# Normalizations and weight parts on GpSimd, all loads in one queue, and a new order at the beginning of a banded attention with a gated feed-forward layer

## The chip, the cores and the metric

The kernel runs on one core of one Trainium2 chip. The metric is the device time of one execution in microseconds: 874.63 us before, the median of three runs (872.39 to 875.89).

## The reference

Attention over 8 batches, 8 heads, 576 positions and 64 dimensions, with a causal window of 64 keys, then a feed-forward layer over the 4608 tokens of 512 channels with 2048 inner ones:

```python
scores = scale * np.matmul(q, k.transpose(0, 1, 3, 2))
mask = (rel >= 0) & (rel < window)            # window = 64
scores = np.where(mask, scores, -1000000000.0)
attn = np.exp(scores - np.max(scores, axis=-1, keepdims=True))
attn = attn / (np.sum(attn, axis=-1, keepdims=True) + 1e-09)
x = np.matmul(attn, v)                        # -> 4608 x 512
h = x @ w_in                                  # 512 x 2048
g = np.where(h >= 1, h, np.where(h <= -1, 0.0, (h + 1) ** 2 / 4))
out = (g @ w_out).astype(np.float32)          # 2048 x 512
```

The weights arrive as float64, q, k and v as float32.

## The kernel before

**Tiles.** The tokens are nine tiles of 512. Each tile is four attention steps of 128 tokens (two query blocks of 64), and then 16 groups f of 128 inner channels: `ffn_in` (L909) multiplies the tile with w_in, a gate follows, `ffn_out` (L960) multiplies with w_out into four PSUM banks `acc`. Every operand of the two products is split into a high part in fp32r and a low part, the remainder; three matmuls (high x high, high x low, low x high) stand for one. Tiles 3 to 8 go in pairs, with seven products where eight would be needed (L840); that part is not touched by more than its numbers.

**Weights.** A group has two units, 0 for w_in and 1 for w_out. A unit of 128 x 512 float64 numbers is 0.5 MB (`raw`). It becomes fp32 by a chain: `w_rest` and `w_sign` on ScalarE (L329, L306), two limits, a shift and a join on VectorE (L310, L322, L333), the high part on ScalarE (`w_high`, L277), the low part on VectorE (`w_low`, L345). The first four groups are loaded in single units, the later twelve in pairs. Each weight is converted once, during tile 0.

**Attention steps.** Step s loads q, k and two v blocks. Steps 0 to 3 add the mask in PSUM by a matmul with the identity (L415), then scores (L421), maximum (L442), exponentials with sums (L449, 16 on ScalarE for the two halves h), inverse (L456, L457), normalization (`att_normalize`, L461, on VectorE for steps 0 to 7), transposes on TensorE (L485, steps 0 to 6) and copies to `ptd` (L277 or L279), then the values (L499), and a high and a low part, `xh` and `xl` (L512). Steps 7 and later transpose on VectorE. L277 and L279 are the copies of the helper `copy` on ScalarE and on VectorE.

**What sets the order.** A planner (class `Plan`) holds every piece of work with a key, a cost in ns for each engine that may do it, what it depends on, and which buffers it takes and gives back. It walks through time on its own costs: of the work that could start on an engine within `PATIENCE`, the smallest key goes first. The order in which it emits is the program order of each engine, and stays that; an engine waits for whatever stands next in its order. A piece marked `shared` does not begin while GpSimd is busy by the plan, nor the other way round. Keys come from tables of numbers: `A_FIRST` for steps 0 to 3, `W_FIRST`, `W_STEP` and `W_LATE` for the weight chain, `W0_KEY` and `W0_STEP` for the weight loads, `L_LEAD` and `V_LATE` for q, k and v.

**Buffers and queues.** q and k have two buffers each, v has four, PSUM has two banks each for `ps_a` and `ps_h`, and four for `acc`. SP issues nearly all transfers, in its program order: a load that waits for a buffer holds up every load behind it. The first k and the first weight unit are issued by ScalarE (the call of `load_k` and `w_load` before `plan.run`).

**Filling.** Eight matmuls on zeros stand at the start (`warm`, L267), and 8 and 4 ahead of the two transposes of step 0 (`FILL`, L483).

## Time and profile before

| | |
|---|---|
| median of three runs | 874.63 us |
| profiled execution | 875.65 us, span 873.8 us |
| mean granted TensorE clock | 0.996 |
| busy: TensorE / VectorE / ScalarE / GpSimd | 861.2 / 648.4 / 501.1 / 179.0 us |
| first 45 us: DMA | 191 to 424 GB/s in pieces of 5 us |
| first L909 | at 24.02 us |
| first GpSimd arithmetic after the masks | at 115.80 us |

The span runs from the first to the last instruction. TensorE's busy time counts matmuls with ends that are modelled, so a stretch of full TensorE has to be compared with the number of matmuls in it. A row of the timeline gives start and length in us, the engine, the line, the operation and the tiles; a "x16" is 16 instructions in a row, and the bracket is the idle time ahead of it and what ended it.

### The profile page before, as it was taken

The page shows a single profiled execution, that of the slowest core. Times are in us where ns is not written, and L with a number is a line of the kernel's source. Part 1 is how long each engine was busy: PE and PEld are TensorE (multiplying, and loading weights), DVE is VectorE, ACT ScalarE, POOL GpSimd, SP SyncE. Part 2 cuts the span into 40 slices and gives each one's busy share as a digit, 9 for nine tenths or more (in the row PEclk, how much of TensorE's full clock was granted, in tenths as well). Part 3 has the DMA queues.
Part 4 walks back from the last instruction along what each step waited for, and adds up shares of the span by engine and source line. Part 5 has one row for each costly group of instructions (what it writes and reads, how often), then busy time and mean ns, then how long its engine had stood idle before and what let it go on. Part 6 is the DMA issues. An engine that isn't in the chain of part 4 may idle for free.

```text
span 873.8 us, 17796 instructions
## 1 busy us (share of the span) xinstructions
PE 861.2 (99%) x6708; PEld 701.4 (80%) x6708; DVE 648.4 (74%) x1282; ACT 501.1 (57%) x1250; POOL 179.0 (20%) x194
## 2 busy tenths in 40 slices
PE   8899999999999999999999999999999999999998
PEld 6788888878787888878877888787888888888886
DVE  6899999987787776797888947888799733333453
ACT  6899976546454556545336845553548733333564
POOL 1000046656332452111111001211121011111000
PEclk9899999999999999999999999999999999999999
DMA  9992126767533314657665407677545045554321
GB/s 318 420 357 93 55 79 223 234 198 234 169 128 128 110 55 140 235 192 229 194 200 190 145 13 239 202 222 216 165 129 180 25 153 166 162 155 146 102 105 48
DMA packets 88116, 147.57 MB, mean 169 GB/s; under 512 B 7392, under 2 KB 36448, under 8 KB 88032
## 3 DMA queue, kind: packets, MB, share of 16 engines
q1 hardware_dynamic: 87600, 145.40, 50.8%
q8 instruction: 53, 0.87, 0.4%
q10 hardware_dynamic: 432, 1.05, 0.3%
q14 instruction: 31, 0.25, 0.1%
HBM read 112.86 MB, written 33.55 MB: 168 GB/s over the span
## 4 chain that ended last, share of the span: by engine, by line
PE 89%; DVE 3%; DMA 3%; ACT 2%; POOL 1%; issue 1%; SPq 0%; ACTq 0%; POOLq 0%; DVEq 0%
PE acc L960 43%; PE ps_h L840 26%; PE ps_h L909 13%; PE ps_a L499 4%; PE ps_a L421 3%; DMA kept<-u 1%; DMA vt<-in_v 1%; ACT sm L449 1%; DMA raw<-in_w 1%; DVE sm L461 1%; DVE ptd L467 0%; DVE a L934 0%; ACT u L329 0%; PE ps_a L485 0%; POOL u L778 0%
## 5 line engine op out<-in xcount | busy, mean ns | idle before, releaser
L960 PE MATMUL acc<-wts,gh 128*128 128x512 f32 x1152 | 360.0, 394 | 0.0
L960 PEld LDWEIGHTS acc<-wts,gh 128*128 128x128 f32 x1152 | 212.8, 188 | 46.8 <-issue 0.3
L960 PE MATMUL acc<-wts,gl 128*128 128x512 f32 x576 | 224.8, 390 | 0.6 <-POOL gl L944 0.6
L944 POOL TENSOR_TENSOR gl<-a,gh 128x512 fp32r<-128x512 f32 (+1 forms) x80 | 103.3, 1292 | 474.4 <-ACT gh L939 399.4
L840 PE MATMUL ps_h<-wts 128*128 128x512 f32 x720 | 180.3, 391 | 0.0
L840 PEld LDWEIGHTS ps_h<-wts 128*128 128x128 f32 x720 | 134.3, 188 | 29.1 <-DVE h L855 0.6
L467 DVE STREAM_TRANSPOSE ptd<-sm 32x256 f32<-32x256 f32 x336 | 146.5, 436 | 5.9
L939 ACT CAST gh<-a 128x512 fp32r<-128x512 f32 (+1 forms) x149 | 89.5, 601 | 89.7 <-DVE a L934 82.2
L855 DVE TENSOR_TENSOR h<-h,ps_h 128x512 f32<-128x512 f32 x120 | 82.0, 684 | 75.2 <-PE ps_h L840 73.8
L909 PE MATMUL ps_h<-xh,wts 128*128 128x512 f32 (+1 forms) x424 | 131.1, 376 | 2.7 <-DVE xh L279 1.7
L960 PEld LDWEIGHTS acc<-wts,gl 128*128 128x128 f32 x576 | 108.1, 188 | 24.3 <-POOL gl L944 1.1
L934 DVE SCALAR_TENSOR_TENSOR a<-a,h 128x512 f32<-128x512 f32 x96 | 66.7, 696 | 63.1 <-ACT a L927 61.7
L922 ACT ACTIVATE a<-h 128x512 f32<-128x512 f32 x96 | 60.3, 631 | 90.9 <-DVE h L855 61.8
L449 ACT ACTIVATE sm<-sm,nm 128x96 f32<-128x96 f32 (+1 forms) x256 | 93.1, 366 | 20.4 <-DVE nm L442 20.4
L909 PEld LDWEIGHTS ps_h<-xh,wts 128*128 128x128 f32 x424 | 78.3, 191 | 17.9 <-DVE xh L279 1.8
L927 ACT ACTIVATE a<-a 128x512 f32<-128x512 f32 (+1 forms) x139 | 85.5, 617 | 4.3
L909 PE MATMUL ps_h<-xl,wts 128*128 128x512 f32 (+1 forms) x212 | 79.1, 373 | 0.4 <-DVE xl L512 0.4
L840 PE MATMUL ps_h<-xs,wts 128*128 128x512 f32 x288 | 73.8, 392 | 0.0
L277 ACT COPY h<-ps_h 128x512 f32<-128x512 f32 x47 | 27.6, 587 | 75.0 <-PE ps_h L840 74.7
L840 PEld LDWEIGHTS ps_h<-xs,wts 128*128 128x128 f32 x288 | 53.7, 188 | 11.5
L922 ACT ACTIVATE a<-ps_h 128x512 f32<-128x512 f32 (+1 forms) x53 | 29.4, 554 | 48.9 <-PE ps_h L909 42.3
L944 DVE TENSOR_TENSOR gl<-a,gh 128x512 fp32r<-128x512 f32 (+1 forms) x69 | 45.6, 662 | 7.8 <-ACT gh L939 7.6
(109 smaller groups left out, 834.4 us busy)
## 6 DMA issues: line engine op xcount, KB each, us to landing
wts<-kept SPq DMA_DIRECT2D x168, 256.0 KB, 3.0
vt<-in_v SPq DMA_DIRECT2D x72, 256.0 KB, 3.4
kt<-in_k SPq DMA_DIRECT2D x35, 384.0 KB, 4.2
raw<-in_w SPq DMA_DIRECT2D x12, 1023.8 KB, 10.0
qt<-in_q SPq DMA_DIRECT2D x36, 256.0 KB, 3.3
spill<-h SPq DMA_DIRECT2D x18, 512.0 KB, 2.9
h<-spill SPq DMA_DIRECT2D x18, 512.0 KB, 3.5
out<-o SPq DMA_DIRECT2D x27, 256.0 KB, 2.3
```

The costliest lines, as they stand in the source:

```text
L449: nc.scalar.activation(sm[:, p, :], (ps if masked else sm)[:, p, :], AF.Exp, bias=nm[:, p:p + 1], scale=scale if masked else 1.0, accum_ou ...
L467: nc.vector.transpose(dst[:, :, r], src[:, :, c * SQ:(c + 1) * SQ])
L499: nc.tensor.matmul(ps[half[h], p, n], lhsT=vt[i][:, c:c + D], rhs=pt[h][:, p, n], start=True, stop=True)
L840: nc.tensor.matmul(ps, lhsT=r[:, part, cp], rhs=x_op(k, xp)[:, cp], start=j in (0, 1, 3, 4) and i == 0 and cp == 0, stop=j in (1, 2, 5, 6) ...
L855: nc.vector.tensor_tensor(out=h[:, to], in0=h[:, of], in1=prods[u, n, b], op=ALU.add)
L909: nc.tensor.matmul(ps, lhsT=wts[f, 0][:, part, c * P:(c + 1) * P], rhs=x[:, c, r], start=(c == 0 and j == 0), stop=(c == NP - 1 and j == 2),)
L922: nc.scalar.activation(gs[t, f, r.start][0], phs[t, f, r.start], AF.Relu, bias=0.5, scale=0.5)
L927: nc.scalar.activation(a, a, AF.Square)
L934: nc.vector.scalar_tensor_tensor(out=a, in0=a, scalar=1.0, in1=ps, op0=ALU.min, op1=ALU.max)
L939: nc.scalar.copy(g[1], g[0])
L944: engine[eng].tensor_tensor(out=g[2], in0=g[0], in1=g[1].bitcast(F32), op=ALU.subtract)
L960: nc.tensor.matmul(acc[t, i], lhsT=g[:, sub], rhs=wts[f, 1][:, part], start=(q == 0 and j == 0), stop=(q == NF - 1 and j == 2),)
```

## The change

The changed program differs in these ways. Line numbers move by 22 to 30: L909 becomes L939, L960 becomes L990, L485 becomes L509, L499 becomes L523, L421 becomes L447, L415 becomes L437, L461 becomes L487, L345 becomes L367.

- 13 normalizations of steps 0 to 6 (all but one) are given to GpSimd, and the low parts of ten weight groups: six single units and four pairs.
- The first k and the first weight unit go through SP with all the others, in a new order.
- The mask products of steps 0 to 3 are a piece of work of their own, which can stand ahead of the arrival of q and k.
- Zeroing of the identity, the masks and `ptd` moves to VectorE and ahead.
- Filling is left to the planner: six matmuls at the start, and as many as fit where it sees TensorE idle before the transposes of steps 0 and 1 and before the first products of tile 0.
- The last tile's last 128 tokens are taken from PSUM whole by ScalarE, not in two halves by VectorE and ScalarE.
- Nearly all numbers of the tables are other ones, those of the later tiles too.

```diff
-W_FIRST = (20.54, -1.96, 1.46, 0.57, -0.16)
-W_STEP = 4 / 3
-L_LEAD = 2
+W_FIRST = (-23.48, 35.42, 28.14, 28.55, 19.15)
+W_STEP = 1.78
+L_LEAD = 16.26
...
-FIRST_LOAD = 0, (0,)
+NORM_POOL = ((0, 0), (0, 1), (1, 0), (1, 1), (2, 0), (2, 1), (3, 0), (3, 1), (4, 0), (4, 1), (5, 1), (6, 0), (6, 1))
+LOW_POOL = ((0, (0,)), (0, (1,)), (1, (0,)), (2, (0,)), (3, (0,)), (3, (1,)), (6, (0, 1)), (7, (0, 1)), (9, (0, 1)), (10, (0, 1)))
...
-NWARM = 8
-FILL = 8, 4
-A_FIRST = (-102.6, -95.58, -95.43, -95)
+NWARM = 6
+FILLED = 3
+FILL_NS = 260
+FILL_SLACK = 500
+A_FIRST = (-144.83, -88.9, -110.73, -84.04)
...
+            if i in self.filled and at < FILL_UNTIL:
+                since = max([idle[e]] + [self.pools[n][turn[n]] for n in takes])
+                self.fills = n = max(0, int((at - since - FILL_SLACK) / FILL_NS))
...
-    def w_low(g):
+    def w_low(g, eng):
         t = ws[g]
-        nc.vector.tensor_tensor(out=t[:, :, 1], in0=us[g], in1=t[:, :, 0].bitcast(F32), op=ALU.subtract)
+        engine[eng].tensor_tensor(out=t[:, :, 1], in0=us[g], in1=t[:, :, 0].bitcast(F32), op=ALU.subtract)
...
-        x = add(key - W_LATE[4], dict(DVE=join), lambda e: w_join(g), [x])
+        x = add(key - W_LATE[4], dict(DVE=join), lambda e: w_join(g), [x], shared=bool(NORM_POOL + LOW_POOL))
...
+            xm = add(key, dict(PE=M_PE), lambda e: att_mask_banks(s, ps), [last["r"]], takes=[ps, ps])
+            needs.append(xm)
...
-                x = add(due + D_LATE[4], NORM[1], lambda e, h=h: att_normalize(s, h, e), [x], shared=True)
+                x = add(due + D_LATE[4], dict(Pool=830) if (s, h) in NORM_POOL else NORM[1], lambda e, h=h: att_normalize(s, h, e), [x], shared=True)
...
-        load_k(0, nc.scalar)
-        w_load(FIRST_LOAD, nc.scalar)
         plan.run()
```

TensorE around the first products of tile 0, before (idt,sm are transposes, ptd,vt values of an attention step, xh,wts the first products):

```order
L909 MATMUL ps_h<-xh,wts 128x256
L485 MATMUL ps_a<-idt,sm 128x128 x12
L499 MATMUL ps_a<-ptd,vt 64x64 x16
L485 MATMUL ps_a<-idt,sm 128x128 x4
L499 MATMUL ps_a<-ptd,vt 64x64 x16
L909 MATMUL ps_h<-xh,wts 128x256
```

The first row is the last matmul of the first block of 12; the transposes and the values of steps 2 and 3 follow, then the second block. The same place now:

```order
L523 MATMUL acc<-ptd,vt 64x64 x16
L509 MATMUL ps_a<-idt,sm 128x128 x4
L523 MATMUL ps_a<-ptd,vt 64x64 x16
L939 MATMUL ps_h<-xh,wts 128x256
...
L939 MATMUL ps_h<-xh,wts 128x256
L509 MATMUL ps_a<-idt,sm 128x128 x8
L939 MATMUL ps_h<-xh,wts 128x256
...
L939 MATMUL ps_h<-xh,wts 128x256
L523 MATMUL ps_a<-ptd,vt 64x64 x16
L990 MATMUL acc<-wts,gh 128x512 x2
```

The values of step 2 now stand ahead of the first block of 12, the second block stands ahead of the values of step 3, and L990 comes right behind these.

GpSimd's first arithmetic was the sums of weights for the later tiles:

```order
L256 MEMSET msk 64x64 x2
L761 TENSOR_TENSOR u<-wts 128x256 x2
L770 TENSOR_TENSOR u<-u 128x128 x3
L761 TENSOR_TENSOR u<-wts 128x256
L778 TENSOR_TENSOR u<-u,o 128x512
```

Now low parts (wts) and normalizations (sm) stand ahead of them:

```order
L278 MEMSET msk 64x64 x2
L367 TENSOR_TENSOR wts<-u,wts 128x512
L487 TENSOR_TENSOR sm<-sm,den 128x512 x2
L367 TENSOR_TENSOR wts<-u,wts 128x512
L487 TENSOR_TENSOR sm<-sm,den 128x512 x4
L367 TENSOR_TENSOR wts<-u,wts 128x512
L487 TENSOR_TENSOR sm<-sm,den 128x512 x2
L367 TENSOR_TENSOR wts<-u,wts 128x512 x3
L487 TENSOR_TENSOR sm<-sm,den 128x512 x2
```

The normalizations of steps 0 to 3 are the eight in the rows of two, four and two.

SP's first transfers, before (ScalarE issues the first k and the first weight unit at the same time; 128x2047 is a weight unit):

```order
L391 DMA qt_146<-in_q 128x512
L400 DMA vt_171<-in_v 128x512
L391 DMA qt_173<-in_q 128x512
L395 DMA kt_177<-in_k 128x768
L400 DMA vt_180<-in_v 128x512
L391 DMA qt_184<-in_q 128x512
L395 DMA kt_215<-in_k 128x768
L296 DMA raw_224<-in_w 128x2047
```

And now:

```order
L318 DMA raw_137<-in_w 128x2047
L413 DMA qt_141<-in_q 128x512
L417 DMA kt_143<-in_k 128x768
L318 DMA raw_151<-in_w 128x2047
L413 DMA qt_160<-in_q 128x512
L417 DMA kt_183<-in_k 128x768
L413 DMA qt_193<-in_q 128x512
L417 DMA kt_198<-in_k 128x768
L318 DMA raw_208<-in_w 128x2047
L422 DMA vt_236<-in_v 128x512
```

A weight unit stands first, a second one ahead of the second step's q and k, and no v is among the first eight. The second pair (qt_160, kt_183) is read by the scores of step 2, the third (qt_193, kt_198) by those of step 1.

More of the change, by code (lines that the diff above doesn't have):

```diff
@@ L271, in banded_attention_then_ffn, with fill @@
     plan = Plan(BUFS)
+    def fill(ps):
+        for _ in range(plan.fills):
+            nc.tensor.matmul(ps, lhsT=idt, rhs=idt, start=True, stop=True)
     add = plan.add
@@ L480, in att_transpose_pe @@
         pts[s, h] = ps = banks_of_heads(pool)
-        if s == 0:
-            for _ in range(FILL[h]):
-                nc.tensor.matmul(ps[:, 0], lhsT=ptd[0][:, 0], rhs=ptd[0][:, 0], start=True, stop=True)
+        fill(ps[:, 0])
         for p in range(NP):
@@ L906, in ffn_in @@
         phs[t, f, r.start] = ps = bank("ps_h")[:, :n]
+        fill(ps[:, :P])
         for c in range(NP):
```

179 lines of the change are left out of this document (97 added, 82 removed).

## The prediction

> **What bounds the kernel now.** I read the page's busy shares and the chain of waits first, then the stretches, then the groups of instructions inside two stretches.
>
> ```profile
> PE 861.2 (99%) x6708; PEld 701.4 (80%) x6708; DVE 648.4 (74%) x1282; ACT 501.1 (57%) x1250; POOL 179.0 (20%) x194
> PE 89%; DVE 3%; DMA 3%; ACT 2%; POOL 1%; issue 1%; SPq 0%; ACTq 0%; POOLq 0%; DVEq 0%
> ```
>
> TensorE is busy for 99% of the span and carries 89% of the chain. But the ends of matmuls are modelled, so "busy" does not say that it ran at its pace. For that I take a pace per instruction from rows where many stand back to back, and count instructions in a stretch:
>
> ```profile
> 48.10 2.72 PE ps_h L909 x12
> ...
> 14.32 0.60 PE L485 MATMUL ps_h<-idt,sm 128*128 128x128 f32 x4
> 14.68 0.71 PE L415 MATMUL ps_a<-mskr,idr 128*128 128x512 f32 x2
> 15.32 1.10 PE L421 MATMUL ps_a<-kt,qt 64*64 64x128 f32 x32
> 16.36 1.15 PE L499 MATMUL acc<-ptd,vt 128*64 128x64 f32 x32
> ```
>
> A matmul of 512 columns takes 2.72 / 12 = 0.227 us, so one of 256 columns 0.113 us. One early attention step costs two mask products (0.71), its scores (1.10), two transposes of four (2 x 0.60) and its values (1.15): 4.2 us. In the window from 60 to 110 us the long matmuls are these:
>
> ```profile
> L909 PE MATMUL ps_h<-xh,wts 128*128 128x512 f32 x64 | 21.5, 397 | 0.0
> L960 PE MATMUL acc<-wts,gh 128*128 128x512 f32 x65 | 20.6, 396 | 0.0
> L960 PE MATMUL acc<-wts,gl 128*128 128x512 f32 x33 | 12.9, 392 | 0.0
> L909 PE MATMUL ps_h<-xl,wts 128*128 128x512 f32 x32 | 12.5, 391 | 0.0
> ```
>
> 194 x 0.227 = 44.0 us of 50, and the attention steps in between fill the rest: here TensorE has nothing left to gain. In the window from 0 to 45 us it is otherwise:
>
> ```profile
> L909 PE MATMUL ps_h<-xh,wts 128*128 128x256 f32 x47 | 10.7, 313 | 2.6 <-DVE xh L279 1.7 <-DVE a L934 0.9
> L909 PE MATMUL ps_h<-xl,wts 128*128 128x256 f32 x23 | 7.2, 312 | 0.4 <-DVE xl L512 0.4
> ...
> L960 PE MATMUL acc<-wts,gh 128*128 128x512 f32 x8 | 2.5, 395 | 0.0
> ...
> L960 PE MATMUL acc<-wts,gl 128*128 128x512 f32 x4 | 1.6, 389 | 0.0
> ```
>
> 70 x 0.113 + 12 x 0.227 + 4 steps x 4.2 = 27.4 us of useful work in 45 us: 17.6 us are lost, and nothing that the change does to VectorE later can be worth more than a share of these. The stretches say what limits there:
>
> ```profile
> 6.70:23.76 17.06, 13.29 (x234) 10.65 (x226) 14.95 (x43) 14.69 (x60) 0.00 (x0) 1.00 0.99 364
> 23.76:30.59 6.83, 6.21 (x30) 5.36 (x32) 6.01 (x16) 5.28 (x23) 0.00 (x0) 0.50 1.05 426
> 30.59:45.00 14.41, 12.62 (x138) 11.42 (x135) 12.53 (x32) 13.60 (x28) 0.00 (x0) 1.00 1.01 417
> 45.00:110.00 65.00, 65.00 (x431) 52.64 (x430) 64.66 (x115) 62.30 (x120) 0.00 (x0) 1.00 0.43 162
> ```
>
> Columns: stretch, length, busy time of PE, PEld, DVE, ACT and POOL, granted clock, DMA share, GB/s. GpSimd does nothing, ScalarE and VectorE are 86% to 88% busy from 6.7 to 23.8 us, and from 23.76 to 30.59 the granted clock is 0.50. From 45 to 110 VectorE is full (64.66 of 65), but so is TensorE: relief for VectorE is hidden there.
>
> **The change part by part.** Each early step runs scores, maximum, exponentials, normalization, transposes, copies, values; all exponentials, most weight conversion and most copies share ScalarE. So I follow ScalarE from the first exponential to the second transposed copy of step 3 (in the kernel before, that copy is on VectorE), behind which the last values of tile 0 stand:
>
> ```profile
> 7.52 0.66 ACT L329 ACTIVATE u<-raw 128x512 uint32<-128x512 uint32 x1 [3.41 <-DMA raw<-in_w]
> ...
> 8.77 0.35 ACT L449 ACTIVATE sm<-ps_a,nm 128x128 f32<-128x128 f32 x1
> ...
> 24.02 0.58 PE L909 MATMUL ps_h<-xh,wts 128*128 128x256 f32 x1 [1.70 <-DVE xh L279]
> ...
> 32.25 0.68 DVE L279 COPY ptd<-ps_a 128x512 f32<-128x512 f32 x1
> 32.99 1.15 PE L499 MATMUL ps_a<-ptd,vt 128*64 128x64 f32 x32 [0.86 <-DVE ptd L279]
> ```
> ```profile
> 8.77:32.93 24.16, 21.09 (x84) 0.86 1.00 383
> ...
> L329 ACT ACTIVATE u<-raw 128x512 uint32<-128x512 uint32 x3 | 2.1, 687 | 0.9 <-DVE nm L442 0.9
> L306 ACT ACTIVATE raw<-raw 128x512 bf16<-128x512 bf16 x3 | 2.0, 678 | 0.1
> L277 ACT CAST wts<-u 128x512 fp32r<-128x512 f32 x3 | 2.0, 669 | 0.0
> ...
> L277 ACT CAST xh<-ps_a 128x512 fp32r<-128x512 f32 x1 | 0.6, 585 | 0.0
> ...
> L939 ACT CAST gh<-a 128x256 fp32r<-128x256 f32 x1 | 0.4, 423 | 0.0
> L927 ACT ACTIVATE a<-a 128x256 f32<-128x256 f32 x1 | 0.4, 417 | 0.0
> ```
>
> The string lasts from 8.77 to 32.93: 21.09 us of work (64 exponentials, six copies of ptd or their like, three each of the weight operations, and so on) and 3.07 us of waits.
>
> *First term, ScalarE's string.* In the new order it holds the same exponentials and three rests and signs, six copies, but one cast of weights less (0.67), one xh less (0.58), and neither the square (0.42) nor the gh (0.42): 21.09 - 2.09 = 19.0 us. It begins later: a rest, a cast and a sign of a second weight unit now stand ahead of the exponentials, 0.69 + 0.67 + 0.68 = 2.0 us. Of these the 3.41 us of idle time before the first rest covers most, since the first weight unit is now the first transfer of the only queue. The second unit lies behind three transfers (0.5 + 0.26 + 0.39 + 0.5 MB at some 0.4 MB a us, from 3 us on), lands near 7.5, and so the exponentials begin near 7.5 + 2.0 = 9.5, which is 0.8 late. Waits I leave at 3.1: the end is at 9.6 + 19.0 + 3.1 = 31.7 against 32.93, **-1.2 us**. Bounds: no wait at all, -4.3; twice the waits, +1.9.
>
> *Second term, what TensorE has done by then.* Before, one block of 12 matmuls of 256 columns precedes the last values; in the new order two do, and the first comes only after the values of step 2. The second block is 12 x 0.113, **-1.4 us**. If the halved clock of the second stretch falls on it, its gain is nothing; that is the upper bound.
>
> *Third term, a new wait.* Right behind the last values now stand six L990 matmuls (L960 before), and they want the first gl. On VectorE it comes after join, limits, low part and gate; behind it the xl of steps 2 and 3 wait. By the order and VectorE's 0.42 to 0.75 us each I find gl about 1.0 us after the last values, of which two gh matmuls cover 0.45: **+0.6 us** (0 to 1.5).
>
> *Fourth term, GpSimd in the string.* Rows for the same work:
>
> ```profile
> L944 POOL TENSOR_TENSOR gl<-a,gh 128x512 fp32r<-128x512 f32 x76 | 100.3, 1320 | 470.6 <-ACT gh L939 395.7 <-PE ps_a L421 53.6 <-issue 9.4
> ...
> L461 POOL TENSOR_TENSOR sm<-sm,den 128x384 f32<-128x384 f32 x6 | 5.0, 828 | 10.0 <-DVE den L457 10.0
> ```
> ```profile
> L461 DVE TENSOR_TENSOR sm<-sm,den 128x512 f32<-128x512 f32 x9 | 5.8, 676 | 0.0
> ```
>
> A normalization of 512 columns lies between 0.83 and 1.32 us on GpSimd; scaling the 384-column row gives 0.828 x 512 / 384 = 1.10, so 0.43 more than 0.68 on VectorE. Only the last of step 3 stands in the string with nothing beside it; the others run under exponentials of the next step. **+0.4 us** (0.1 to 0.6, and 4 x 0.6 = 2.4 if each step feels it). The 13 normalizations and the low parts (six of 512, four of 1024 columns) take 13 x 0.68 + 6 x 0.68 + 4 x 1.36 (twice the 512) = 18 us off VectorE; after 45 us TensorE's full stretch hides this. If that cover were gone, at most the losses of 30.59 to 45 would shrink. On GpSimd it is 13 x 1.1 + 6 x 1.32 + 4 x 2.64 = 33 us over some 100 us, on an engine that had nothing to do.
>
> *Loads.* SP now issues everything, and step 2's q and k stand ahead of step 1's. There are two q buffers, so step 1's q waits until the scores of step 0 have freed one, and what stands behind it on SP (its k, the third weight unit, the first v) waits too. The transfers of such an issue in the kernel before:
>
> ```profile
> 7.53 0.33 SPq L391 DMA_DIRECT2D qt<-in_q  x1
> ...
> kt<-in_k SPq DMA_DIRECT2D x1, 384.0 KB, 3.6
> qt<-in_q SPq DMA_DIRECT2D x1, 256.0 KB, 2.7
> ```
>
> The scores of step 0 want the first three transfers (near 6) and four mask products (1.4), so they are done near 8.6; step 1's k, issued 0.4 later, lands near 9.0 + 3.6 = 12.6, and its scores end near 13.7; the maxima near 15. ScalarE comes to these exponentials only after the first ones (2.8 us from 9.6 on), a cast, a rest, a sign and two copies, near 16: covered, with about 1 us to spare. Cost 0; without the cover up to 2 us. Later weights come up to 6 us later or earlier than before, but at two blocks of 2.72 us a group TensorE wants group 6 only near 34 + 6 x 5.4 = 66 us: 0.
>
> *The end.*
>
> ```profile
> 869.49 0.59 ACT L277 COPY o<-acc 128x512 f32<-128x512 f32 x1
> ...
> 870.17 0.42 DVE L279 COPY o<-acc 128x256 f32<-128x256 f32 x1 [4.32 <-PE acc L960]
> 870.62 0.37 ACT L277 COPY qt<-acc 128x256 f32<-128x256 f32 x1 [0.55 <-DVE o L279]
> ```
>
> The last tile is now taken whole: 870.17 + 0.59 = 870.76 instead of 870.99, **-0.2 us**. Between 110 and 868 the new numbers reorder work that TensorE bounds; I take 0, within 2 us either way.
>
> Sum: -1.2 - 1.4 + 0.6 + 0.4 - 0.2 = -1.8 us. The profiled execution took 875.65 us (span 873.8 and 1.85 around it), so 873.85; it lies 1.0 above the median of the runs, 874.63, so on that scale **872.8 us**.
>
> **The rivals.** *Much shorter beginning.* GpSimd and the order take away ScalarE's 3.07 us of waits altogether (the bound of the first term), and VectorE, freed, also gives back some 1 us of the PE waits of 0.9 and 1.7 us in the rows above. Then -1.8 - 3.1 - 1.0 = -5.9: **868.7 us**. For it: the waits were on transposes, maxima and joins, the very things that are moved. Against: every copy still waits for a longer normalization.
>
> *GpSimd and VectorE hold each other up.* If two-operand work on one delays the other, the three joins and the low parts of the first 34 us are late by a GpSimd instruction each, and casts behind them: about four times half of 1.1 us, 2 us. The gain is gone: **874.6 us**. Against: the mean of 1.32 us for 76 GpSimd operations leaves little room for waiting, though there the planner kept them apart from VectorE's, as it does in the new kernel. [...]
>
> *The clock falls early, on the string (slower).* Between the scores of step 0 (end 8.6) and those of step 1 (from 12.6) TensorE has one pair of mask products, and there are now nine filling matmuls where there were 20. Before, a stretch that ended in the wait of 1.70 us was followed by 6.83 us at 0.50. If that comes between 13.5 and 20.4, two blocks of transposes, scores and values (4.1 us) take twice as long, of which the transposes delay ScalarE's copies and with them all later exponentials: about +3; if another low stretch follows at the first block of 256 columns, +2.2 more. -1.8 + 5.2 = +3.4: **878.0 us**. [...]
>
> **How the numbers follow.** Forecast 0.50, much shorter beginning 0.28, hold-up 0.12, early fall of the clock 0.10. A measurement of this kernel tells about 0.5% (4.4 us) from no change, so the borders are 870.3 and 879.0. Faster: the second case and a little of the first, 0.30; slower: the worse part of the last case and what I did not think of in the long middle, 0.09; the rest, 0.61. The likeliest case alone spans 870.5 to 875 (its bounds on waits, added half-way). The range takes in most of the second case and the last: 867.5 to 877.5.
>
> **What would show it.** In the new profile: the first exponential near 9.5 us, the values of step 3 near 32 us (first term); two blocks of 256-column matmuls before them (second); a PE wait for gl just behind (third); GpSimd normalizations of 1.1 us (fourth); useful work in 0 to 45 us of about 29 us instead of 27.4; 45 to 110 full as before. I am wrong if the stretch after 45 us changes by more than 2 us, if 0.50 stands anywhere before 20 us, or if the values of step 3 come before 30 or after 35 us.

## The result and the profile after

The changed kernel is slower: 884.97 us (median of four runs, 881.35 to 885.22) against 875.26 for the kernel before in the same runs. The ratio is 1.0107 with a 95% interval of 1.0072 to 1.0143 (written in brackets from here on). I had forecast 872.8, with 867.5 to 877.5 as the range.

The profiled execution of the changed kernel is the quickest of its four (881.35 us, span 879.6). Its trace therefore shows 5.8 us of the slowdown (879.6 - 873.8), and about 4 of the 9.7 us between the medians lie outside it. The first line of its page, and then three of its stretches, with the columns of the prediction:

```profile
PE 860.9 (98%) x6686; PEld 697.0 (79%) x6686; DVE 661.1 (75%) x1266; ACT 491.3 (56%) x1233; POOL 218.0 (25%) x225
```
```profile
0.00:45.00 45.00, 36.03 (x432) 29.77 (x433) 39.11 (x93) 36.91 (x120) 17.00 (x26) 0.96 0.92 331
60.00:100.00 40.00, 37.25 (x303) 28.32 (x301) 39.63 (x61) 32.39 (x62) 13.76 (x7) 1.00 0.46 173
200.00:240.00 40.00, 37.28 (x334) 29.39 (x333) 36.11 (x74) 22.30 (x68) 23.25 (x29) 1.00 0.77 231
```

The same two later stretches of the kernel before:

```profile
60.00:100.00 40.00, 40.00 (x236) 32.44 (x235) 39.90 (x68) 37.69 (x73) 0.00 (x0) 1.00 0.33 126
200.00:240.00 40.00, 40.00 (x347) 32.23 (x347) 32.47 (x69) 20.96 (x59) 22.75 (x29) 1.00 0.63 191
```

Although 18 us of work went from VectorE to GpSimd, VectorE's busy time rose from 648.4 to 661.1 us. It is about as full from 60 to 100 us as before (39.63 of 40 us, before 39.90), but TensorE is no longer full beside it (37.25 of 40).

Busy time of TensorE hides short waits, so I use the measure of the prediction: in each stretch I count the matmuls, multiply by their paces (0.227 and 0.113 us for 512 and 256 columns, 0.60 / 4 a transpose, 1.10 / 32 and 1.15 / 32 an early score and value; later scores of 96 columns by the row that follows, 3.0 / 192 = 0.016), and call the rest of the stretch **lost**. The row is from the groups between 190 and 226 us of the changed kernel:

```profile
L447 PE MATMUL ps_a<-kt,qt 64*32 64x96 f32 x192 | 3.0, 248 | 0.0
```

Lost time of TensorE in us, for the two kernels and the experiments on which the conclusions rest (their edits follow):

| stretch | before | after | e1 | e3 | j4 | h3 | h1 | h2 | n1 | n2 |
|---|---|---|---|---|---|---|---|---|---|---|
| 0 to 60 | 18.5 | 16.0 | 18.1 | 16.2 | 19.6 | 21.5 | 17.4 | 19.4 | 17.2 | 17.9 |
| 60 to 80 | -0.2 | **1.8** | 0.0 | 1.3 | 2.6 | -0.4 | 1.4 | -0.2 | 1.4 | 0.2 |
| 80 to 100 | 0.4 | **3.3** | 2.6 | 1.5 | 2.0 | 3.6 | 3.7 | 0.4 | 3.8 | 2.4 |
| 100 to 200 | 2.5 | 1.5 | 1.5 | 3.5 | 1.3 | 2.6 | 1.3 | 2.6 | 2.7 | 2.7 |
| 200 to 240 | 0.8 | **3.9** | 4.2 | 0.9 | 1.1 | 5.0 | 3.7 | 1.1 | 1.0 | 1.4 |
| 240 to 450 | 4.1 | 3.9 | 4.1 | 4.3 | 3.9 | 3.9 | 4.8 | 6.2 | 11.1 | 5.2 |
| 450 to 700 | 3.8 | **5.2** | 5.2 | 4.7 | 4.1 | 5.4 | 3.8 | 3.2 | 5.4 | 3.8 |
| median, less that of before | 0 | +9.7 | +7.7 | +5.0 | +5.4 | +12.1 | +7.9 | +2.0 | +14.4 | +6.0 |

The rows of the changed kernel account for the difference of the spans: 2.5 us gained before 60 us, 4.9 lost from 60 to 100, 1.0 gained from 100 to 200, 3.1 lost from 200 to 240, and 1.2 more after that, 5.7 of 5.8 in all. The gain before 60 us is not a firm number. Eleven profiled kernels share that beginning's order and assignment or differ from it only in a few operations; they lost 16.0 to 18.3 us there, 17.5 in the mean, and three with the old beginning lost 16.2, 18.5 and 19.4. A part of this is the clock of the single execution. The kernel before had a clock of 0.50 from 23.76 to 30.59 us in its profile; e3, which begins with the same instructions and lost the 16.2, had 1.00 over its whole span.

**From 60 to 100 us** VectorE's short operations have become long. VectorE's timeline in the changed kernel:

```profile
41.36 0.68 DVE L468 TENSOR_REDUCE nm<-sm 128x4 f32<-128x512 f32 x1
...
63.79 0.44 DVE L332 TENSOR_SCALAR raw<-raw 128x1024 int16<-128x1024 int16 x1
...
64.73 2.47 DVE L332 TENSOR_SCALAR raw<-raw 128x1024 uint16<-128x1024 uint16 x1
...
91.78 0.68 DVE L464 SCALAR_TENSOR_TENSOR sm<-ps_a,msk 128x512 f32<-128x512 f32 x1
92.39 2.00 DVE L344 TENSOR_SCALAR raw<-raw 128x1024 uint16<-128x1024 uint16 x1
```

and GpSimd's:

```profile
41.30 1.30 POOL L367 TENSOR_TENSOR wts<-u,wts 128x512 fp32r<-128x512 f32 x1 [5.54 <-ACT wts L299]
...
64.53 2.39 POOL L367 TENSOR_TENSOR wts<-u,wts 128x1024 fp32r<-128x1024 f32 x1 [5.90 <-ACT wts L299]
...
91.49 2.61 POOL L367 TENSOR_TENSOR wts<-u,wts 128x1024 fp32r<-128x1024 f32 x1 [4.83 <-ACT wts L299]
```

A limit or a shift of a weight (L332, L344) of 128 x 1024 takes 0.42 to 0.44 us by itself. In these rows, where a low part runs on GpSimd, it takes 2.0 to 2.5 us, and ends just behind the low part (64.53 + 2.39 = 66.92; 64.73 + 2.47 = 67.20). The masking at 91.78, which reads PSUM, keeps its 0.68 us beside the last of these GpSimd operations, and so does the maximum at 41.36, which reads SBUF, beside the first. Over the first 110 us the groups of VectorE tell the sum, before:

```profile
L345 DVE TENSOR_TENSOR wts<-u,wts 128x1024 fp32r<-128x1024 f32 (+1 forms) x18 | 17.7, 983 | 0.1
L310 DVE TENSOR_SCALAR raw<-raw 128x1024 int16<-128x1024 int16 (+3 forms) x38 | 13.8, 364 | 0.7 <-ACT raw L306 0.5
L461 DVE TENSOR_TENSOR sm<-sm,den 128x512 f32<-128x512 f32 x13 | 8.6, 678 | 0.0
L322 DVE TENSOR_SCALAR raw<-raw 128x1024 uint16<-128x1024 uint16 (+1 forms) x18 | 6.4, 361 | 0.1
L456 DVE TENSOR_SCALAR den<-den 128x4 f32<-128x4 f32 x14 | 2.3, 164 | 0.4 <-ACT sm L449 0.4
L444 DVE TENSOR_SCALAR nm<-nm 128x4 f32<-128x4 f32 x8 | 1.4, 170 | 0.3
```

and after:

```profile
L332 DVE TENSOR_SCALAR raw<-raw 128x1024 int16<-128x1024 int16 (+3 forms) x36 | 17.6, 488 | 3.7 <-ACT raw L328 3.5
L344 DVE TENSOR_SCALAR raw<-raw 128x1024 uint16<-128x1024 uint16 (+1 forms) x18 | 10.6, 588 | 0.3
L367 DVE TENSOR_TENSOR wts<-u,wts 128x1024 fp32r<-128x1024 f32 (+1 forms) x7 | 7.7, 1099 | 0.0
L482 DVE TENSOR_SCALAR den<-den 128x4 f32<-128x4 f32 x14 | 4.2, 299 | 0.1
L470 DVE TENSOR_SCALAR nm<-nm 128x4 f32<-128x4 f32 x8 | 4.2, 521 | 0.3
L487 DVE TENSOR_TENSOR sm<-sm,den 128x512 f32<-128x512 f32 x1 | 0.7, 695 | 0.0
```

Low parts and normalizations fell from 26.3 to 8.4 us: 17.9 off, as forecast. The four kinds of one-input operations rose from 23.9 to 36.6 us for two operations fewer: 12.7 come back as stretching. Copies and casts (L279, now L301) rose from 3.5 to 7.4 us by the sums of their rows, because the new order gives more of them to VectorE. What is left of 18 us is 1.3.

**From 200 to 240 us** the wait is this one (waits of TensorE, changed kernel: 2.7 us in two waits, the longest 2.0; the kernel before has none there):

```profile
PE ps_h L939 <- DVE a L964: 2.7, 2, 2.0
```

VectorE's timeline there. Before, a gate (L934) comes every 5 to 8 us, here:

```profile
193.37 0.68 DVE L934 SCALAR_TENSOR_TENSOR a<-a,ps_h 128x512 f32<-128x512 f32 x1
...
201.13 0.67 DVE L934 SCALAR_TENSOR_TENSOR a<-a,ps_h 128x512 f32<-128x512 f32 x1
...
207.15 0.69 DVE L934 SCALAR_TENSOR_TENSOR a<-a,ps_h 128x512 f32<-128x512 f32 x1
```

After, the gates (L964) stand unevenly: here are two pairs with 13 us between them, and a later gate, at 222.68, comes 10 us behind the one ahead of it:

```profile
190.95 0.69 DVE L964 SCALAR_TENSOR_TENSOR a<-a,ps_h 128x512 f32<-128x512 f32 x1
...
192.14 0.69 DVE L964 SCALAR_TENSOR_TENSOR a<-a,ps_h 128x512 f32<-128x512 f32 x1
...
203.24 1.00 DVE L790 TENSOR_TENSOR u<-wts 128x256 f32<-128x256 f32 x1 [1.27 <-DMA kept<-u]
204.16 1.53 DVE L487 TENSOR_TENSOR sm<-sm,den 128x384 f32<-128x384 f32 x2
205.62 0.68 DVE L964 SCALAR_TENSOR_TENSOR a<-a,ps_h 128x512 f32<-128x512 f32 x1
...
206.58 0.64 DVE L964 SCALAR_TENSOR_TENSOR a<-a,ps_h 128x512 f32<-128x512 f32 x1
...
222.68 0.69 DVE L964 SCALAR_TENSOR_TENSOR a<-a,ps_h 128x512 f32<-128x512 f32 x1
```

The first products have two PSUM banks, so TensorE can be two gates ahead and no more; it waits for the gates that come late, those at 205.62 us (2.0 us) and at 222.68 us (0.7 us).

### The profile page after: what moved, and what is told of

It reads as the page before. It is cut to its first block, busy times and chain, and to the rows that moved or that the text cites. A ratio compares the mean times of both kernels' runs of the same rounds, so it can differ in the third digit from the quotient of the medians.

```text
span 879.6 us, 17828 instructions
## 1 busy us (share of the span) xinstructions
PE 860.9 (98%) x6686; PEld 697.0 (79%) x6686; DVE 661.1 (75%) x1266; ACT 491.3 (56%) x1233; POOL 218.0 (25%) x225
## 5 line engine op out<-in xcount | busy, mean ns | idle before, releaser
L990 PE MATMUL acc<-wts,gh 128*128 128x512 f32 x1152 | 358.1, 392 | 0.0
L990 PEld LDWEIGHTS acc<-wts,gh 128*128 128x128 f32 x1152 | 214.2, 188 | 45.7
L990 PE MATMUL acc<-wts,gl 128*128 128x512 f32 x576 | 225.1, 391 | 0.2
L974 POOL TENSOR_TENSOR gl<-a,gh 128x512 fp32r<-128x512 f32 (+1 forms) x79 | 101.1, 1281 | 425.1 <-ACT gh L969 417.9
L939 PE MATMUL ps_h<-xh,wts 128*128 128x512 f32 (+1 forms) x424 | 131.0, 376 | 2.9 <-DVE a L964 2.7
L990 PEld LDWEIGHTS acc<-wts,gl 128*128 128x128 f32 x576 | 108.1, 188 | 25.5 <-DVE gl L974 2.6
L964 DVE SCALAR_TENSOR_TENSOR a<-a,h 128x512 f32<-128x512 f32 x96 | 66.1, 690 | 50.0 <-ACT a L957 48.1
L939 PEld LDWEIGHTS ps_h<-xh,wts 128*128 128x128 f32 x424 | 77.2, 188 | 20.3 <-DVE a L964 3.6
L957 ACT ACTIVATE a<-a 128x512 f32<-128x512 f32 (+1 forms) x135 | 83.1, 618 | 4.0
L939 PE MATMUL ps_h<-xl,wts 128*128 128x512 f32 (+1 forms) x212 | 78.5, 370 | 0.0
L974 DVE TENSOR_TENSOR gl<-a,gh 128x512 fp32r<-128x512 f32 (+1 forms) x70 | 48.4, 694 | 6.9 <-ACT gh L969 6.7
L475 ACT ACTIVATION_READ_ACCUMULATOR sm<-sm,nm 128x1 f32 x256 | 48.0, 188 | 0.0
```

Of the source, the lines that this page charges most:

```text
L475: nc.scalar.activation(sm[:, p, :], (ps if masked else sm)[:, p, :], AF.Exp, bias=nm[:, p:p + 1], scale=scale if masked else 1.0, accum_ou ...
L939: nc.tensor.matmul(ps, lhsT=wts[f, 0][:, part, c * P:(c + 1) * P], rhs=x[:, c, r], start=(c == 0 and j == 0), stop=(c == NP - 1 and j == 2),)
L957: nc.scalar.activation(a, a, AF.Square)
L964: nc.vector.scalar_tensor_tensor(out=a, in0=a, scalar=1.0, in1=ps, op0=ALU.min, op1=ALU.max)
L974: engine[eng].tensor_tensor(out=g[2], in0=g[0], in1=g[1].bitcast(F32), op=ALU.subtract)
L990: nc.tensor.matmul(acc[t, i], lhsT=g[:, sub], rhs=wts[f, 1][:, part], start=(q == 0 and j == 0), stop=(q == NF - 1 and j == 2),)
```

## The experiments

Times are medians; differences are against the kernel before, run alongside. The changed kernel's own interval is wide (6.3 to 12.5 us over the kernel before), so 2 us against it are not clear of the noise, and the conclusions rest on the traces too.

### Does GpSimd hold VectorE off?

**e1**, the four low parts of 1024 columns on VectorE at their places in the changed kernel:

```diff
     def w_low(g, eng):
         t = ws[g]
+        if len(g[1]) == 2:
+            eng = "DVE"
```

> The changed kernel with the low parts of the four pairs (groups 6, 7, 9, 10) emitted on VectorE at the places where the plan had put them for GpSimd; nothing else differs. Theory 1 (GpSimd holds VectorE off: each of these four 2.4 us operations keeps one VectorE operation of 0.4 us waiting for 1.6 to 2.1 us, 7.1 us in all on a VectorE that is full from 60 to 100 us): VectorE gets 4 x 1.22 = 4.9 us of work and loses 7.1 us of waits, so TensorE's loss from 60 to 100 us falls from 5.1 to 2 to 3.5 us, and the time by 1.5 to 3 us. Theory 2 (the new order and the later loads make the loss from 60 to 100 us): the loss grows by VectorE's extra work, 2 to 5 us slower.

882.38 us, 1.0083 [1.0068, 1.0098]. The loss from 60 to 80 us is gone (0.0), that from 80 to 100 mostly stays (2.6 against 3.3). Both together are 2.5 us less than in the changed kernel, as theory 1 expected; the medians differ by 2.0 us in the same direction.

**e2**, the same low parts on GpSimd in pieces of 256 columns:

```diff
+        if len(g[1]) == 2 and eng == "Pool":
+            for j in range(2):
+                for c in range(2):
+                    n = slice(c * DM // 2, (c + 1) * DM // 2)
+                    nc.gpsimd.tensor_tensor(out=t[:, j, 1, n], in0=us[g][:, j, n], in1=t[:, j, 0, n].bitcast(F32), op=ALU.subtract)
+            return
```

> The changed kernel with each of the four pair low parts cut into four GpSimd operations of 256 columns (0.74 us each instead of one of 2.4 us). Theory 1 (a lock held for the whole instruction): no VectorE operation waits longer than some 0.75 us there, the four waits of 1.6 to 2.1 us become 4 x 0.4 to 0.75 if a waiting VectorE operation gets its turn between two pieces; the time falls by 2 to 4 us. [...] Theory 2 (order and loads): no change.

882.64 us, 1.0088 [1.0071, 1.0106]. GpSimd and, over the same time, VectorE:

```profile
66.28 4.96 POOL L371 TENSOR_TENSOR wts<-u,wts 128x256 fp32r<-128x256 f32 x4 [5.91 <-ACT wts L299]
```
```profile
66.48 0.82 DVE L332 TENSOR_SCALAR raw<-raw 128x1024 uint16<-128x1024 uint16 x1
67.33 0.84 DVE L344 TENSOR_SCALAR raw<-raw 128x1024 uint16<-128x1024 uint16 x1
```

A VectorE operation now waits for one piece, 0.82 in place of 2.0 to 2.5 us, and GpSimd's four pieces take 4.96 us here, and 3.2 to 3.5 us the three other times, where one operation took 2.4 to 2.6. So in these rows the two take turns, operation by operation. The loss from 60 to 100 us fell little, from 5.1 to 4.3 us: the lengths of single operations speak for theory 1, the time does not decide.

**e3**, the kernel before, with eight subtractions on GpSimd whose results nobody reads:

```diff
+        if g[0] in (6, 7, 9, 10):
+            for j in range(2):
+                s = wpool.tile([P, 480], BF16, name="spare", tag="spare")
+                nc.gpsimd.tensor_tensor(out=s, in0=t[:, j, 0, :480].bitcast(F32), in1=t[:, j, 1, :480].bitcast(F32), op=ALU.subtract)
```

> The kernel before with GpSimd work that nobody needs: behind the low parts of groups 6, 7, 9 and 10, two subtractions of 480 columns each of the finished weights into a spare tile (1.2 us each, 9.6 us in all, on a GpSimd that is idle there). Nothing waits for them. Theory 1: VectorE operations that meet them take up to 1.2 us longer, 4 to 8 us in all between 60 and 95 us where VectorE is full, and the kernel gets 2 to 6 us slower. Theory 2: GpSimd beside VectorE costs nothing: within 0.7 us of before.

879.71 us, 1.0056 [1.0037, 1.0075]: 5 us for GpSimd work on which nothing waits. In the trace 2.6 us more than before are lost from 60 to 100 us, where this work stands; some 2 us more appear later, where the two kernels do the same, and stay unexplained. The timeline of GpSimd and that of VectorE:

```profile
72.11 4.20 POOL L349 TENSOR_TENSOR spare<-wts 128x480 bf16<-128x480 f32 x2 [4.69 <-DVE wts L345]
```
```profile
72.80 1.86 DVE L333 TENSOR_TENSOR u<-u,raw 128x1024 uint16<-128x1024 uint16 x1
...
75.72 0.87 DVE L310 TENSOR_SCALAR raw<-raw 128x1024 int16<-128x1024 int16 x1
```

A join of 1.37 us took 1.86, a limit of 0.42 took 0.87, and GpSimd's pair grew from 2.6 us to 4.2. This is the cleanest test: order, loads and readers are those before, and only the engine beside VectorE is busy.

**j4 and h3** separate the offload from the order. j4 is the kernel before with only the assignment:

```diff
-        nc.vector.tensor_tensor(out=t[:, :, 1], in0=us[g], in1=t[:, :, 0].bitcast(F32), op=ALU.subtract)
+        (nc.gpsimd if g in LOW_POOL else nc.vector).tensor_tensor(out=t[:, :, 1], in0=us[g], in1=t[:, :, 0].bitcast(F32), op=ALU.subtract)
...
+        if (s, h) in NORM_POOL:
+            eng = "Pool"
```

> The kernel before with its order, loads and numbers, and only the 13 normalizations and ten low parts given to GpSimd where they stand. Together with the order alone (886.5 against 874.4, of which the middle has 2.0) and the changed kernel (10 more than before) this fills a table of two by two. If offload and order add, the offload is worth about -2 us: 872.5. Theory 1 (held off) says that VectorE gets some 18 us off and 8 to 14 us back as stretching, so -2 to +2 from that alone. If an offload that wasn't planned for makes the readers of low parts and normalizations wait on an engine in order, it is slower: 877 or more.

h3 is the changed kernel with all of this work on VectorE, at the places where the new plan has it:

```diff
-        engine[eng].tensor_tensor(out=t[:, :, 1], in0=us[g], in1=t[:, :, 0].bitcast(F32), op=ALU.subtract)
+        nc.vector.tensor_tensor(out=t[:, :, 1], in0=us[g], in1=t[:, :, 0].bitcast(F32), op=ALU.subtract)
...
+        if s < PE_STEPS:
+            eng = "DVE"
```

> The changed kernel with its order, loads and middle, but the normalizations of the first seven steps and all low parts on VectorE, where they stand in the plan: no GpSimd instruction until the first gl and sums. Theory 1 (GpSimd's operations hold VectorE's off): no VectorE weight operation of 16 bits is longer than 0.8 us before 100 us, and VectorE gains 14 us of stretching and takes on 18 us of work: from 0 to 100 us within 3 us of the changed kernel either way; so the offload as a whole was worth at most a few us. Theory 2 (the new order and the loads are what costs in 60 to 100 us): the loss of 4 to 5 us there stays although no GpSimd work is beside it and VectorE's operations have their usual lengths. The loss from 200 to 240 us stays by both.

j4 took 880.1 us, 1.0055 [1.0038, 1.0071]; h3 took 886.5, 1.0134 [1.0117, 1.0151]. Offload alone +5, order alone +12, both together +10. So the parts do not add: in the old order the offload costs 5 us, in the new order it costs nothing (2.4 us less than without it, not clear of the noise). In h3 the lengths are the usual ones again (groups of VectorE to 110 us):

```profile
L332 DVE TENSOR_SCALAR raw<-raw 128x1024 int16<-128x1024 int16 (+3 forms) x36 | 13.0, 362 | 4.1 <-ACT raw L328 3.6 <-ACT sm L475 0.3
L344 DVE TENSOR_SCALAR raw<-raw 128x1024 uint16<-128x1024 uint16 (+1 forms) x17 | 6.1, 361 | 0.2
```

Yet its loss from 80 to 100 us stays (3.6), and it loses 3 us more than the kernel before up to 60 us. A part of h3's losses is the clock in this execution: in the mean it was 0.83 from 0 to 20 us and 0.91 from 20 to 40 (before 1.00 and 0.83), 1.00 from there to 200 us, and 0.992 over the whole span of 885.5 us, so some 2 us (885.5 x 0.008 - 20 x 0.17 - 20 x 0.09 = 1.9) are lost to it behind 200 us. In j4 it is otherwise: besides stretching, TensorE waits for low parts that GpSimd now makes later (waits from 40 to 100 us):

```profile
PE ps_h L913 <- POOL wts L347: 3.3, 3, 1.4
PE ps_h L913 <- DVE a L938: 1.7, 2, 1.3
```

**j1**, six copies of steps 4 to 6 back on ScalarE, which is busy for only 32.4 of 40 us from 60 to 100:

```diff
-        copy(eng, ptd[pt_of(s, h)], pts.pop((s, h)))
+        copy("ACT" if 4 <= s < PE_STEPS else eng, ptd[pt_of(s, h)], pts.pop((s, h)))
...
-        copy(eng, xt[t][0][:, :, i * SB:(i + 1) * SB], vals[s])
+        copy("ACT" if 4 <= s < PE_STEPS else eng, xt[t][0][:, :, i * SB:(i + 1) * SB], vals[s])
```

> The changed kernel, with the six copies and casts of attention steps 4 to 6 (ptd and xh) on ScalarE, where before two of these were on VectorE and now all six are (57 to 81 us, 0.68 us each, 4.1 us together). Theory 5 (VectorE is the bound from 60 to 100 us, and the new order gives back to it in copies a part of what GpSimd took off): ScalarE, busy for 32.4 of 40 us there, takes them in its gaps, and the loss of 4 to 5 us from 60 to 100 falls to about 2: 2 to 3.5 us less than the changed kernel. Rival 5b (what is late there is single operations that are held off, not the sum of work): less than 1 us.

883.64 us, 1.0093 [1.0076, 1.0111]; the loss from 60 to 100 us is 5.2, as before the edit. Theory 5 fell: 4 us less work on VectorE there is worth nothing that shows.

### The middle

**h1 and h2** change the numbers of the middle alone (pace and lead of gates, sums and the ninth group on; some 20 table entries), back to those before in h1, to the new ones in h2:

```diff
-S_LATE = 2.36
-S_LATER = 3.68
...
-EARLY_2 = 2.75
+S_LATE = 3
+S_LATER = 3
...
+EARLY_2 = 1.5
```

> The changed kernel, with the new numbers of the middle (gate lead and steps, due times of the sums, the order of o and of the ninth group on) as they stood before. Theory 4 (the new middle is worse for VectorE's gates: TensorE loses 3.9 us from 200 to 240 us where it lost 0.8, and 1.4 us more from 450 to 700): that 3 us and most of the 1.4 come back, so 3 to 4.5 us less than the changed kernel, 880.5 to 882 on the scale on which it took 885, and the wait for the gate of 2.0 us near 204 us is gone. Rival 4b (the loss near 204 us is a late echo of the beginning, since groups and gates arrive out of step from there): nothing comes back, within 1 us of the changed kernel. The stretch from 60 to 100 us keeps its 4 to 5 us of loss by both.

> The kernel before, with only the new numbers of the middle. Theory 4: 3 to 4.5 us more than before (877.7 to 879.2 on a scale of 874.7), the loss standing from 200 to 240 us and from 450 to 700. Rival 4b: within 1 us of before. Theory 1 (GpSimd holds VectorE off) says nothing of this run, since no GpSimd work is added.

h1 took 882.33 us, 1.009 [1.0075, 1.0105]; h2 876.43, 1.0021 [1.001, 1.0032], which is 2 us over the kernel before. The 1.4 us from 450 to 700 us come back in h1 (3.8), so they belong to these numbers. In h2 no such loss appears there (3.2); there the price stands from 240 to 450 us (6.2 against 4.1). The loss from 200 to 240 us stays in h1 and is not in h2: it is not from these numbers, and in this theory 4 was wrong.

**h4**, h1 and e1 together, and **j5**, these and j1:

> The changed kernel with both supposed causes undone: the low parts of the four groups of two units on VectorE at the same places, and the numbers of the middle as before. The normalizations and the six low parts of one unit stay on GpSimd, and the new order, loads and end stay. If the two causes add, 2.5 (low parts) and 3 to 4.5 us (middle) come off: 878 to 879.5 on the scale on which the changed kernel took 885; what is left above the kernel before (874.7) is then the holding up by the smaller GpSimd operations. If it is not slower than before by more than 1 us, those smaller ones cost nothing that the gain of 2.4 us before 60 us doesn't pay.

> The changed kernel with three things undone: low parts of groups of two units on VectorE, the numbers of the middle as before (these two together 880.75), and the six copies of steps 4 to 6 on ScalarE. If the copies add to the other two, 2 us less, 878.5 to 879; the rest above the kernel before would then be the loss from 200 to 240 us (3.5 against 0.8). Rival: with the low parts back on VectorE it is full again and ScalarE's copies come too late: 880 or more.

880.75 us, 1.0069 [1.0053, 1.0086], and 880.67, 1.0062 [1.0042, 1.0083]. The low parts and the middle take off 3.4 of the 9.7 us together, the copies again nothing that shows.

**e5**, all the first sums of weights (L790) on GpSimd, and **j2**, 31 of GpSimd's sums between 187 and 236 us cut to 8 columns, which leaves out most of these sums of weights for tiles 3 to 8:

```diff
-        engine[eng].tensor_tensor(
+        nc.gpsimd.tensor_tensor(
             out=t[:, 2 * i:2 * i + 2], in0=w_[:, 0, c].bitcast(F32), in1=w_[:, 1, c].bitcast(F32), op=ALU.add
```
```diff
+        return 8 if 45 < len(sums_done) <= 76 else P
...
-        engine[eng].tensor_tensor(out=t[:, out], in0=t[:, x], in1=t[:, y], op=op)
+        m = short(eng)
+        engine[eng].tensor_tensor(out=t[:, out, :m], in0=t[:, x, :m], in1=t[:, y, :m], op=op)
```

> The changed kernel with all sums of weights of the helper at L790 on GpSimd, also those that the plan gave to VectorE; order otherwise the same. Theory 3 (near 203 us such a sum heads VectorE's order and waits 1.3 us for the write of kept weights, two normalizations and a gate stand behind it, and TensorE waits 2.0 and 0.7 us for that gate): the waits of TensorE on the gate near 206 us go, and the time falls by 2 to 3 us. If the gate is late for another reason: within 1 us, or slower, since GpSimd gets some 10 us more work.

> The changed kernel, with the 31 sums that GpSimd does from 187 to 236 us cut to 8 of 128 columns, so that they take nearly no time (the weights for tiles 3 to 8 are then wrong in places; no other work is left out). Theory 6 (near 204 and 222 us the gates are late because GpSimd's sums hold off VectorE's sums and normalizations there, 3.1 us of stretching after against 0.5 before): no VectorE operation is stretched by over 0.2 us there, and the loss from 200 to 240 us falls from 3.9 to about 1.3: 2 to 3 us less in total. Rival 6b (the order of VectorE's work there, gates behind sums that wait for a transfer): less than 1 us comes back and the wait for the gate near 204 us stays.

884.16 us, 1.011 [1.009, 1.013], and 883.82, 1.0097 [1.008, 1.0114]. From 200 to 240 us they lost 4.3 and 3.4. So neither a sum at the head of VectorE's order nor the sums on GpSimd make this loss; theories 3 and 6 fell.

**n1**, one number for tiles 1 and 2, the lag of the second products behind the first:

```diff
         if t < PLAIN - 1 or q < NF - 2:
-            return O_LAG
+            return O_LAG if t == 0 else 2.66
```

> The changed kernel, with one number put back for tiles 1 and 2 alone: the lag of the second products behind the first (5.84 now, 2.66 before). Up to about 150 us the order is that of the changed kernel. Theory 9 (with the long lag the gates come in pairs, with 7 to 8 us of other VectorE work ahead of each pair, and TensorE, which has two banks for the first products, waits for the first gate of a pair): the pairs are gone, the waits for gates near 204 and 222 us too, and the loss from 200 to 240 us falls from 3.9 to about 1, so 3 us less than the changed kernel: 882. Rival 9b (a late echo of the beginning): the loss stays, 884 to 885. From 60 to 100 us nothing changes by either.

888.35 us, 1.0163 [1.0145, 1.0182]: slower still. But the loss from 200 to 240 us is gone (1.0), the gates from 197 us on stand 5.6 to 7.5 us apart, and TensorE waits for none of them. The price has moved to the start of tiles 3 and 4, where TensorE waits for sums of x (waits from 335 to 360 us):

```profile
PE ps_h L869 <- DVE wts L586: 3.1, 1, 3.1
PE ps_h L869 <- DVE wts L301: 1.4, 1, 1.4
```

The waits are 4.5 of the 7.2 us that n1 loses more from 240 to 450 us (11.1 against 3.9). Behind the longer wait TensorE is slower than its pace, 353.63 - 351.76 = 1.87 us for four matmuls of 512 columns, 0.47 each in place of 0.227:

```profile
351.76 2.07 PE L869 MATMUL ps_h<-wts 128*128 128x512 f32 x4 [3.13 <-DVE wts L586]
353.63 0.63 PE L869 MATMUL ps_h<-xs,wts 128*128 128x512 f32 x1
```

The granted clock of this execution was 0.992 in the mean, that of the changed kernel 0.998; how much of the other 2.7 us is due to it was not measured.

**n2**, n1's line, h1's numbers and e1's low parts together:

> The changed kernel with three causes undone: low parts of the groups of two units on VectorE (2.5 us), the numbers of the middle as before (2 us), and the lag of the second products as before for tiles 1 and 2 (3 us by theory 9). The first two together took 880.75. If the third adds, 877.5 to 878.5, and what is left above the kernel before (874.7) is the loss of 2.4 us from 80 to 100 us and what is held up by smaller GpSimd operations. By rival 9b: 880.5.

879.95 us, 1.007 [1.0055, 1.0084]. The stretches became what the three causes say (0.2, 1.4 and 3.8 in the rows of 60 to 80, 200 to 240 and 450 to 700 us), but 1 us of the gain from 200 to 240 stands again from 100 to 200 us (2.7 against 1.5), and 1.1 us from 240 to 450. In total it is no better than h4, and 6.0 of the 9.7 us remain: the three causes are seen in their stretches, but undoing them brings back less than half of the slowdown.

**k1 to k4** put back more numbers at once, to separate the later attention steps from those of tile 1:

```diff
-A_NEXT = -16.59
+A_NEXT = 1.26
...
-O_LAG = 5.84
+O_LAG = 2.66
...
-        lk = key - L_LEAD
+        lk = key - (L_LEAD if s < 8 else 2)
```

That is k1, on top of h1, with the patience of each engine and the lead of the v loads put back too. k2 puts back A_STEP, A_SPAN and A_LEAD too (4.77, 10 and 5), k3 adds e1's edit, and k4 also takes the normalizations of steps 4 to 6 to VectorE.

> The changed kernel with the numbers of the middle as before (882.3 by itself), and with the lead of the q, k and v loads from step 8 on, the patience of each engine and the lead of the outputs as before too. Theory 7 (from 200 to 240 us the gates stand in pairs behind long stretches of other VectorE work, since the scores of tile 2 and 3 come early): the gates stand apart again, the loss from 200 to 240 falls from 3.7 to about 1, and the total is 2.5 us below that of the middle undone: about 880. Rival 7b (a late echo of the beginning, whatever the order): the loss stays, 882 or more. The loss from 60 to 100 stays by both.

> As the run with the later steps' numbers put back, and the spacing, span and lead of the attention steps of tile 1 (steps 4 to 7) as before as well. Theory 8 (the loss of 2.4 to 4 us from 80 to 100 us that every kernel with the new order has comes from where these steps stand): it falls to 1 or less, and what is left from 60 to 100 us is the holding up by the low parts, about 2.5: some 2 us less than the run before it, 878. Rival 8b (weights and loads in their new order): it stays, 880.

> As the run before it, and the low parts of the groups of two units on VectorE. If the three causes (held-up VectorE 2.5, later steps 2.5 and middle 2, steps of tile 1 2) add, 10 us less the gain of the beginning remain: within 2 us of the kernel before, 873 to 876. If a cause is missing, 877 or more.

> As the run before it, and the normalizations of steps 4 to 6 on VectorE too, so that GpSimd takes only the eight normalizations of steps 0 to 3 and the six low parts of one unit, all but one before 45 us. The candidate for a kernel that beats both: the gain of the new beginning, 2 us, without what follows. Theory 1 (what GpSimd takes is worth something only before 45 us): 872 to 875, at or below the kernel before. Rival: with nothing off VectorE from 45 to 110 us it is full and the new order costs 3 us there as in the order alone: 877 or more.

904.89, 902.22, 900.54 and 900.4 us: 25 to 30 over the kernel before, where 872 to 880 were expected. `O_LAG` and the patience also act in tile 0, and its order became another one. In k1, for one, TensorE waits for a weight's high part (waits from 40 to 60 us):

```profile
PE ps_a L509 <- ACT wts L299: 7.1, 1, 7.1
```

Its granted clock was 0.985 in the mean, against 0.996 in the kernel before.

These four runs decide nothing on tile 1's steps, and nothing on the candidate that was to beat both kernels. No version beat the kernel before.

## Why the prediction was wrong

**The views that the prediction prints were read rightly, and the beginning went much as forecast.** The stretch of ScalarE's string in the changed kernel, from the first exponential to the end of the second copy of step 3, and a shorter stretch within it:

```profile
9.91:32.52 22.61, 16.78 (x251) 13.57 (x252) 21.57 (x52) 20.02 (x82) 11.66 (x11) 0.92 1.00 368
...
13.54:16.94 3.40, 3.40 (x26) 2.32 (x28) 3.26 (x7) 2.44 (x5) 2.65 (x3) 0.50 0.97 375
```

*First term*, -1.2: the string began at 9.91 (forecast 9.6) and ended at 32.52 (forecast 31.7), so -0.4. Its work was 20.02 us (forecast 19.0) and its waits 2.59 (forecast 3.1), so the rival of a much shorter beginning, which took all waits away, did not happen. *Second term*, -1.4: two blocks of 256-column matmuls do stand ahead of the last values. *Third term*, +0.6: absent, as TensorE's timeline shows:

```profile
33.26 1.15 PE L523 MATMUL ps_a<-ptd,vt 128*64 128x64 f32 x32
34.34 0.73 PE L990 MATMUL acc<-wts,gh 128*128 128x512 f32 x2
34.91 0.39 PE L990 MATMUL acc<-wts,gl 128*128 128x512 f32 x1
```

The second products follow the values with no wait for gl. *Fourth term*: GpSimd's 13 normalizations took 1.13 us in the mean, forecast 1.10. Useful work in 0 to 45 us is 68 x 0.113 + 18 x 0.227 + 4 x (0.71 + 1.20 + 1.15) + 5 x 1.10 = 29.5 us against 27.4, counted as in the prediction; forecast about 29. *Loads*: step 1's k ended its wait at 12.12 us (forecast 12.6). The third rival was there in part: after that wait of 3.22 us the clock was 0.50, once and early, for 3.4 us from 13.54 (the second row above), which is 3.4 x 0.5 = 1.7 us of TensorE. The place that I gave it, 13.5 to 20.4 us, and the 5.2 us that I added up from it were estimates that no view of before shows. So one of the signs of being wrong came true, 0.50 ahead of 20 us; the values of step 3, at 33.26 us, stayed within their bounds. The gain of the beginning survived it in this execution; over eleven kernels it is 0.5 us in the mean (17.5 against 18.0 of three) and not resolved. The forecast starts from a profile with 6.83 us at 0.50; e3's profile, with the same beginning and a clock of 1.00 throughout, shows that this differs between executions.

*The end*, -0.2: the whole copy stands there as forecast (1.27 us for the last two); too small to tell.

**Two steps failed. The first is "the 13 normalizations and the low parts [...] take 18 us off VectorE [...]; after 45 us TensorE's full stretch hides this".** I asked only whether relief was worth anything, and put its worth at 0. It was no relief: 12.7 of 17.9 us came back as stretching and 3.9 as copies, and in a stretch where both engines were full, with single operations late by up to 2 us, TensorE lost 4.9 us more from 60 to 100 us. About half of that goes with the four low parts on GpSimd (2.5 us less in e1); the other half belongs to the new order (below).

**The rival "GpSimd and VectorE hold each other up" was the right effect, at the wrong place and on the wrong operations.** I let it act on joins and low parts in the first 34 us and gave it 2 us; that two-operand work would be held up was my assumption, and the 2 us an estimate that no run shows. In the changed kernel it acts on the limits and the shift (2.0 to 2.5 us in place of 0.42 to 0.44) and the small operations on 128 x 4 (0.30 and 0.52 us in the mean in place of 0.16 to 0.17), all `TENSOR_SCALAR` with one input in SBUF, through 100 us. In the old order GpSimd work that nobody reads costs 5 us (e3), of which the trace shows 2.6 in the stretch of this work; in j4 late low parts are a part of the 5 us; in the changed kernel its whole price was not measured apart from the order. Its place was open to view: the planner keeps GpSimd's pieces apart from those marked `shared`, the joins, normalizations, low parts and sums, and limits and shift carry no such mark. The rows that the prediction prints show no such wait, but the trace of the kernel before has some after 115 us. There an operation on 128 x 8 that takes 0.17 us by itself took 0.70 us and ended just behind a GpSimd operation (VectorE, then GpSimd):

```profile
243.54 0.70 DVE L456 TENSOR_SCALAR den<-den 128x8 f32<-128x8 f32 x1
```
```profile
243.28 0.92 POOL L536 TENSOR_TENSOR u<-u 128x256 f32<-128x256 f32 x1
```

Likewise, 13 of the 15 normalizations of 128 x 384 on VectorE that began beside a GpSimd `TENSOR_TENSOR` took 0.7 to 1.65 us, where one by itself takes 0.55. So the rival could have been read in the trace before the change. How long a VectorE operation took followed the GpSimd operation beside it: 2.0 to 2.5 us beside one of 2.4 to 2.6 us (changed kernel), 0.82 and 0.84 us beside pieces of which four took 3.2 to 5.0 us together (e2). And in the old order the offload alone went 5 us the wrong way (j4).

**The second step that failed is the middle, "I take 0, within 2 us either way".** Its numbers alone cost 2 us (h2). The loss of 3 us from 200 to 240 us comes with gates that stand far apart; n1, which puts back the lag of the second products alone, takes away both. So from 200 us on the new numbers cost 4.3 us in the changed kernel's trace (3.1 and 1.2), behind 1.0 gained from 100 to 200 us: nearly as much as the stretch from 60 to 100 us. That TensorE "bounds" this stretch does not make the order harmless: with two banks for the first products a gate that is 13 us behind the last one stopped it for 2.0 us.

**What is open.** The 2.4 to 4 us from 80 to 100 us stand in every kernel with the new order, with or without GpSimd work (h3, e1, j5), and in none with the old order and nothing on GpSimd (the k runs, with still another order, are left aside). With the low parts back on VectorE the longest wait there is that of an attention step's scores for VectorE's `xl`, 1.0 to 1.2 us in e1, h4, j5 and n2, and 1.2 in h3; in e1:

```profile
PE ps_a L449 <- DVE xl L538: 1.2, 1, 1.2
```

Which of the numbers of the order makes them late was not found. That the order costs because it was made for a VectorE with less to do is argued from h3 and j4, not shown. With three causes undone 6.0 of the 9.7 us remain (n2). And about 4 us of the slowdown lie in executions that were not profiled.
